# One fixed order of single steps for the front and the first tile, a third raw buffer, and low words on ScalarE

## The chip, the core and the metric

The kernel runs on one core of a Trainium2 chip. TensorE (PE) multiplies matrices, VectorE (DVE), ScalarE (ACT) and GpSimd (POOL) work on tiles in SBUF, and SyncE (SP) issues all the DMAs. The metric is the device time of one launch in microseconds (us), lower being better.

## The reference

Two layers. The first is an mLSTM: per batch and head a state `C` of 40 x 40 and a vector `n` are carried over 768 steps, with gates that are stabilised by a running maximum. The second is a feed-forward layer on its output, whose activation is the square of a clipped line.

```python
for t in range(S):                     # B, H, S, D = 4, 8, 768, 40
    m_new = np.maximum(f_gate[:, :, t] + m, i_gate[:, :, t])
    f_stab = np.exp(f_gate[:, :, t] + m - m_new)
    i_stab = np.exp(i_gate[:, :, t] - m_new)
    C = f_stab[..., None, None] * C + i_stab[..., None, None] * np.einsum('bhd,bhe->bhde', vt, kt)
    n = f_stab[..., None] * n + i_stab[..., None] * kt
    denom = np.maximum(np.abs(np.einsum('bhd,bhd->bh', n, qt)[:, :, None]), 1.0)
    y[:, :, t] = 1 / (1 + np.exp(-o_gate[:, :, t])) * np.einsum('bhde,bhe->bhd', C, qt) / denom
h = x @ w_in                           # x: 3072 x 320, w_in: 320 x 2048
g = np.where(h >= 1, h, np.where(h <= -1, 0.0, (h + 1) ** 2 / 4))
out = g @ w_out                        # 2048 x 320
```

The weights `w_in` and `w_out` arrive as 64-bit floats, and the kernel makes 32-bit floats of them from the raw words.

## The kernel before

Time is cut into 6 chunks of 128 steps, and 4 batches by 6 chunks make 24 **sequences** n = 0 to 23. Each goes through the attention: `prep` (mask and exponents of the decay matrix `Abc`, on POOL and ACT), `score` (q times k on PE, times the decay matrix on DVE, in two halves), `main` (a read of the state, the main product, the denominator `z`, the output `y`, its transposes, and its high and low parts `xh` and `xl`), and a carry that renews the state `C`. Four sequences give 512 tokens, one **tile** j of the feed-forward layer, of which there are 6. A tile has 16 blocks fc: `mm1` is the first product into a bank `psh` (8 matmuls on high and low parts), ACT makes `relu` and its square from it, DVE the largest of that and the bank (`r`), which frees the bank; there are two. `mm2` is the second product into four banks `pso`. In tile 0 it is a plain f32 product (`ow`, `r`); from tile 1 on it is one in three parts (`oh`, `ol`, `gh`, `gl`). Since `LAG` is 2, `mm2` of a block comes two blocks after its `mm1`.

The weights come in 16 parts, 8 of each, each for two blocks. `load_w` issues the load into a raw buffer `wraw` (two of them), and `convert` makes the floats: ACT shifts the magnitude (`mg`), DVE writes the sign (high half of `win` or `ow`), POOL the low words, DVE bounds `mg` and joins both; for w_in ACT then makes the high part `wh` and DVE the low part `wl`. The order `W_ORDER` (lines 431 to 435) runs one part of w_in ahead. `split_next` (line 788) converts a part whole, as `DUE` asks, and issues the load of the part after the next.

The **front** (lines 799 to 861) is written out in `STEPS`, a word for a step: a load (`L..`), filler matmuls on zeros (`w2`), scores (`s0`), exponents by halves (`x20`, `x21` for sequence 2), and the like. In it `InOrder` (line 71) keeps each engine's instructions in the order written. After the front the order on each engine is the scheduler's, which takes priorities from the program's order: `slot(i)` (line 727) runs the steps that the table `plan` has for block i, and `behind(...)` puts some of them after named instructions. SP issues DMAs strictly in its order; each uses one of eight semaphores in turn, so a DMA also waits for the eighth before it.

Of the kernel before, what the change touches and what calls it, by code (L numbers as in the profile page):

```python
# [34 lines left out]
PLAIN_FC = 16  # L35
# [5 lines left out]
EARLY = 8  # L41
# [5 lines left out]
JOINED = (4, 5, 6, 7)  # L47
ST = 0
# [3 lines left out]
DUE = lambda fc: 3 + fc  # L52
# [18 lines left out]
class InOrder:  # L71
# [7 lines left out]
    def __getattr__(self, name):  # L79
        def call(*args, **kwargs):  # L80
            if not InOrder.on or self.last is None:
# [17 lines left out]
def mlstm_ffn_kernel(ctx, tc, qk, qn, vk, og, fi0, fi, fib, w_in, w_out, cst, out):  # L99
# [83 lines left out]
    def load_batch():  # L183
        mb["row"] = mid.tile([NSEQ, 2, 4 * L], F32, name="fi_r")
# [14 lines left out]
    def batch_sums():  # L199
        a, m = mb["fi"][:, 0, :], mb["m"]  # L200
        ah = mb["ah"] = mid.tile([P, L], F32, name="ah_b")
        ac = mb["ac"] = mid.tile([P, L], F32, name="ac_b")
# [169 lines left out]
    def words(out, raw):  # L372


# [4 lines left out]
        out = out.rearrange("p k f -> p (k f)").bitcast(I32)  # L379
        halves = out.bitcast(U16).rearrange("p (f w) -> p f w", w=2)  # L380
# [18 lines left out]
    def load_w(kind, i):  # L399
        if kind == "in":  # L400
            n = 2 * P
            raw = stage.tile([P, 3, 2 * n], I32, name="wraw", bufs=2)
            at = nc.sync.dma_start(raw.rearrange("p k f -> p (k f)"), w_in[i])
        else:
            raw = stage.tile([P, 2, 2 * DM], I32, name="wraw", bufs=2)
# [4 lines left out]
    def convert(kind, i):  # L410
        raw = raws.pop((kind, i))
        if kind == "in":
            sl = slice(2 * i * P, 2 * (i + 1) * P)
            w = stage.tile([P, 3, 2 * P], F32, name="win", bufs=1)
            words(w, raw)
            yield
            yield from split(wh[:, :, sl], wl[:, :, sl], w)
        else:
            of[i] = ow.tile([P, 656], F32, name="ow")[:, :2 * DM].rearrange("p (k e) -> p k e", k=2)
            words(of[i], raw)  # L420
            if 2 * i >= PLAIN_FC:
                yield
                yield from split_out(i)
# [114 lines left out]
    def prep(n):  # L538

        c, b = divmod(n, B)  # L540
        t = T[n]
        select(n)
        if n not in JOINED:
            yield
# [4 lines left out]
        scale1(n)  # L549
        load_v(n + 1)  # L550
        yield
# [58 lines left out]
    def carry_on(n, t):  # L610

        c, b = divmod(n, B)
        kp = psum_a()
        for gi, h0 in enumerate(GROUPS):
            nc.tensor.matmul(kp[0:120, gi * 3 * D1:(gi + 1) * 3 * D1], t["kn"][:, h0 * D:(h0 + 3) * D],
                             t["v2"][:, h0:h0 + 3, :], start=True, stop=True)
        Cn = st.tile([120, 3, 3 * D1], F32, name="C", bufs=5)
# [3 lines left out]
        if c > 0:  # L621
            C = state[b]
            nc.gpsimd.tensor_tensor(out=C, in0=C, in1=dec[:, :, b, c:c + 1].broadcast_to([120, 3, 3 * D1]),
                                    op=ALU.mult)
            nc.vector.tensor_tensor(out=Cn, in0=Cn, in1=C, op=ALU.add)
        state[b] = Cn

    def first(n):

        load_v(n)  # L630
        scale2(n)
        yield
        carry_on(n, T.pop(n))
        yield

    def main(n):

        c, b = divmod(n, B)
        t = T.pop(n) if n >= B else T[n]
        g = gates_of(n)  # L640
        sg = sig[c][:, b, :]
        M = t["A"]
        if c > 0:
            C = state[b]
            ip = psum_a()
            for gi, h0 in enumerate(GROUPS):
                o = 6 - h0 if gi == 2 else 0
                nc.tensor.matmul(ip[:, (h0 + o) * D1:(h0 + 3) * D1], t["qn"][:, gi, :], C[:, gi, o * D1:3 * D1],
                                 start=True, stop=True)
            hv = wk.tile([P, H, D1], F32, name="hv", bufs=2)  # L650
            iv = ip[:, :H * D1].rearrange("p (h d) -> p h d", d=D1)
            nc.vector.tensor_tensor(out=hv, in0=iv, in1=g[:, 2, :].unsqueeze(2).broadcast_to([P, H, D1]), op=ALU.mult)
        up = psum_a()
        hot(up)
        if n < SPLIT_FROM or b == B - 1:
# [13 lines left out]
        uv = up[:, :H * D1].rearrange("p (h d) -> p h d", d=D1)  # L669
        if c > 0:  # L670
            nc.vector.tensor_tensor(out=hv, in0=uv, in1=hv, op=ALU.add)
        else:
            hv = uv
        if n >= B:
            load_A(n + NA)
        yield
# [4 lines left out]
        nc.vector.reciprocal(out=z, in_=z)  # L681
        sz = wk.tile([P, H, D], F32, name="sz", bufs=1)
# [4 lines left out]
        if 0 < c < NC - 1:  # L687
            carry_on(n, t)
# [7 lines left out]
        if c == 0:  # L696
            yield
# [6 lines left out]
        mark["x", "act"] = nc.scalar.copy(xh[:, :, cs], xv)  # L704
# [266 lines left out]
```

## Time and profile before

| what | value |
|---|---|
| median of 3 runs | 518.27 us (517.52 to 518.61) |
| span of the profiled execution | 516.2 us |
| busy: PE, DVE, ACT, POOL | 490.7, 343.0, 289.1, 135.9 us |
| chain that ended last | PE 85%, DVE 6%, ACT 5%, DMA 3% |
| idle of ACT's relu for PE, of DVE's largest for ACT | 111.4, 71.3 us |
| one load: w_in part, w_out part, decay matrix, gate sig | 768, 640, 512, 640 KB |
| one load: half of q and k, v and k, q | 160, 324, 180 KB |

The span runs from the first to the last instruction, and the timed runs take in a little around it. Busy PE time is not PE at its peak, since matmuls are pipelined and their ends are modelled; so the time from the start of one group to the start of the next tells more than a duration. Nearly all instructions are recorded by the helper `InOrder` and stand on its lines 82 and 85; the tiles tell them apart. Times are counted from the span's start.

### The profile page before, as it was taken

How to read it: one execution, taken by the hardware profiler on the slowest of the kernel's cores; microseconds unless marked ns; L12 is line 12 of the kernel's file. 1: busy time of each engine (PE TensorE's matmuls, PEld its weight loads, DVE VectorE, ACT ScalarE, POOL GpSimd, SP SyncE). 2: the span in 40 equal slices, each digit the busy share in tenths (PEclk: the TensorE clock that was granted, in tenths of full speed). 3: DMA queues.
4: the chain of work that ended last, by engine and by line, in shares of the span. 5: the costliest groups of instructions: out<-in, count | busy, mean ns of one | idle time of the engine just before them, and what ended most of it. 6: DMA issues, size and time to landing. Idle time of an engine off the chain costs nothing.

```text
span 516.2 us, 8817 instructions
## 1 busy us (share of the span) xinstructions
PE 490.7 (95%) x3396; PEld 419.4 (81%) x3399; DVE 343.0 (66%) x621; ACT 289.1 (56%) x560; POOL 135.9 (26%) x136
## 2 busy tenths in 40 slices
PE   8985999889898999999999998999999999999996
PEld 3763877778677989988889988889888889988986
DVE  4789896679758776759696657756756745444332
ACT  4525884436087555676645567555377554455553
POOL 2324531343433333323142314403230210000000
PEclk8987999979999999999999999999999999999999
DMA  8868664364441303323223423113522000010001
GB/s 227 257 183 307 161 189 138 115 193 150 131 146 40 107 27 96 118 66 111 65 78 83 133 80 118 68 53 96 170 81 77 16 1 1 0 52 1 1 2 51
DMA packets 29646, 51.48 MB, mean 100 GB/s; under 512 B 10060, under 2 KB 19940, under 8 KB 29604
## 3 DMA queue, kind: packets, MB, share of 16 engines
q1 hardware_dynamic: 29604, 50.92, 32.4%
q8 instruction: 27, 0.44, 0.4%
q14 instruction: 15, 0.12, 0.1%
HBM read 46.80 MB, written 4.04 MB: 98 GB/s over the span
## 4 chain that ended last, share of the span: by engine, by line
PE 85%; DVE 6%; ACT 5%; DMA 3%; issue 1%; SPq 0%; ACTq 0%; DVEq 0%
PE pso L82 33%; PE psh L82 33%; PE psa L82 15%; ACT Abc L82 1%; PE pso L85 1%; DMA raw<-in_qk 1%; ACT L82 1%; PE psa L85 1%; DVE ow L82 1%; DMA wraw<-in_w_in 1%; PE psh L85 1%; ACT r L82 1%; DVE win L82 1%; DMA out<-r 1%; ACT sig L82 0%
## 5 line engine op out<-in xcount | busy, mean ns | idle before, releaser
L82 ACT ACTIVATE r<-psh,half 128x512 f32<-128x512 f32 x96 | 65.4, 685 | 111.7 <-PE psh L82 111.4
L82 DVE SCALAR_TENSOR_TENSOR r<-psh,r 128x512 f32<-128x512 f32 x96 | 65.8, 686 | 71.5 <-ACT r L82 71.3
L82 PE MATMUL psh<-xh,wh 128*128 128x512 f32 x288 | 104.3, 418 | 6.7 <-DVE r L82 6.1
L82 PE MATMUL pso<-oh,gh 128*128 128x320 f32 x320 | 100.6, 317 | 2.4 <-ACT gh L82 2.1
L82 PE MATMUL psh<-xh,wl 128*128 128x512 f32 x288 | 99.8, 401 | 0.0
L82 PE MATMUL pso<-ow,gh 128*128 128x320 f32 x320 | 99.2, 312 | 0.0
L82 PE MATMUL pso<-oh,gl 128*128 128x320 f32 x320 | 94.0, 311 | 1.6 <-DVE gl L82 1.6
L82 DVE TENSOR_TENSOR gl<-r,gh 128x512 fp32r<-128x512 f32 x80 | 62.2, 779 | 40.5 <-ACT gh L82 40.4
L82 ACT CAST gh<-r 128x512 fp32r<-128x512 f32 x80 | 49.4, 618 | 51.0 <-DVE r L82 50.4
L82 PEld LDWEIGHTS pso<-oh,gh 128*128 128x128 f32 x320 | 60.1, 188 | 7.4 <-ACT gh L82 2.5
L82 PEld LDWEIGHTS psh<-xh,wl 128*128 128x128 f32 x288 | 55.2, 192 | 13.1 <-DVE wl L85 0.4
L82 PEld LDWEIGHTS psh<-xh,wh 128*128 128x128 f32 x288 | 51.8, 194 | 15.2 <-DVE r L82 6.8
L82 PEld LDWEIGHTS pso<-ow,gh 128*128 128x128 f32 x320 | 60.2, 188 | 2.8
L82 PE MATMUL psh<-xl,wh 128*128 128x512 f32 x192 | 62.3, 405 | 0.0
L82 ACT ACTIVATE r<-r 128x512 f32<-128x512 f32 x96 | 60.4, 632 | 2.5
L82 PEld LDWEIGHTS pso<-oh,gl 128*128 128x128 f32 x320 | 58.9, 188 | 2.1 <-DVE gl L82 1.9
L82 ACT ACTIVATE Abc<-Abc,nA 128x128 f32<-128x128 f32 x160 | 49.9, 391 | 0.2
L82 POOL TENSOR_TENSOR v<-vk,G 128x328 f32<-128x328 f32 x36 | 30.6, 856 | 58.3 <-issue 45.9
L82 PEld LDWEIGHTS psh<-xl,wh 128*128 128x128 f32 x192 | 36.8, 192 | 8.6
L82 PE MATMUL pso<-ow,r 128*128 128x320 f32 x128 | 38.5, 443 | 0.5 <-DVE ow L82 0.5
L82 POOL TENSOR_SCALAR_AFFINE_SELECT Abc<-Abc 128x1024 f32<-128x1024 f32 x20 | 25.4, 1275 | 48.3 <-DMA Abc<-a_d 46.1
L82 POOL TENSOR_TENSOR m<-m 128x1024 bf16<-128x1024 f32 x12 | 24.4, 2037 | 46.4 <-DVE m L82 46.4
(203 smaller groups left out, 681.0 us busy)
## 6 DMA issues: line engine op xcount, KB each, us to landing
Abc<-a_d SPq DMA_DIRECT2D x20, 512.0 KB
raw<-in_qk SPq DMA_DIRECT2D x48, 160.0 KB
vk<-in_vk SPq DMA_DIRECT2D x20, 324.0 KB
wraw<-in_w_in SPq DMA_DIRECT2D x8, 768.0 KB
wraw<-in_w_out SPq DMA_DIRECT2D x8, 640.0 KB
sig<-in_og SPq DMA_DIRECT2D x6, 640.0 KB
out<-r SPq DMA_DIRECT2D x24, 160.0 KB
qn<-in_qn SPq DMA_DIRECT2D x20, 180.0 KB
```

Source lines behind the costliest of these rows:

```text
L82: r = getattr(self.engine, name)(*args, **kwargs)
L85: r = getattr(self.engine, name)(*args, **kwargs)
```

## The change

The written order goes on to the end of tile 0. `STEPS` gets some 250 words more, such as `mm.2`, `relu.2`, `max.2`, `out.2` for the steps of a block, `w.1` for the next single step of the conversion of weight part 1, `W.3` for a load, `carry.0`, `prep.4`, `score.4`, `main.4` for the next step of a sequence's; the generators now yield after nearly each instruction. `--` stands where the banks of tile 0 are taken. Low words go from POOL to ACT, `wraw` has three buffers, the parts alternate between w_in and w_out, and two small tiles of the gates (`ah`, `ac`) share a buffer with `fi_r`. The main loop begins at tile 1, whose steps by block are the same in number and place.

```diff
+    "w2 E3 A3 x30 e v2.0 w2 s3 v3 w.1 y1 x31 t0 m30 m31 w2 u2 z1 y2 w2 v.1 u3 v.3 t1 z2 qk.4 v2.1 w.2 W.3 y3 w2 "
+    "v.2 t2 z3 qk.5 w.2 og.1 v2.3 w.2 W.4 t3 d g1 -- A.4 v2.2 carry.0 carry.3 A.5 mm.0 mm.1 w.2 relu.0 w.2 carry.3 "
+    "w.3 w.3 max.0 carry.1 prep.4 tail.1 w.2 carry.0 carry.1 out.0 v.4 W.5 relu.1 carry.2 A.6 w.2 w.3 w.3 sig.1 "
...
-    def words(out, raw):
+    def words(new, raw):
...
         nc.scalar.activation(mg, hi.bitcast(F32), AF.Abs, scale=65536.0)
+        yield
+        out = new().rearrange("p k f -> p (k f)").bitcast(I32)
+        halves = out.bitcast(U16).rearrange("p (f w) -> p f w", w=2)
+        nc.scalar.activation(halves[:, :, 0], quarter[:, :, 1], AF.Copy, scale=1 / 8192, bias=-4095.5 / 8192)
+        yield
+        nc.vector.tensor_scalar_max(mg, mg, TINY)
+        yield
         nc.vector.tensor_scalar(out=halves[:, :, 1], in0=quarter[:, :, 3], scalar1=0x8000, scalar2=None,
                                 op0=ALU.bitwise_and)
-
-        nc.gpsimd.tensor_scalar(out=halves[:, :, 0], in0=quarter[:, :, 1], scalar1=1 / 8192, scalar2=-4095.5 / 8192,
-                                op0=ALU.mult, op1=ALU.add)
-        nc.vector.tensor_scalar_max(mg, mg, TINY)
+        yield
         nc.vector.scalar_tensor_tensor(out=out, in0=mg.bitcast(I32), scalar=3, in1=out,
                                        op0=ALU.logical_shift_left, op1=ALU.bitwise_or)
+        yield
...
-            raw = stage.tile([P, 3, 2 * n], I32, name="wraw", bufs=2)
+            raw = stage.tile([P, 3, 2 * n], I32, name="wraw", bufs=3)
...
-    W_ORDER = [("in", 0)]
-    for i in range(NFC // 2):
-        if i + 1 < NFC // 2:
-            W_ORDER.append(("in", i + 1))
-        W_ORDER.append(("out", i))
+    W_ORDER = [(kind, i) for i in range(NFC // 2) for kind in ("in", "out")]
...
+    def tile0(what):
+        kind, n, *_ = what.split(".") + [0]
+        n = int(n)
+        if kind == "mm":
+            block[n] = mm1(0, n)
+        elif kind == "relu":
+            gs[n] = relu(block[n])
+        elif kind == "max":
+            gs[n] = largest(block[n], gs[n]),
+        elif kind == "out":
+            mm2(ops[0], n, *gs.pop(n))
+        elif kind == "w":
+            weights(n)
+        elif kind == "W":
+            load_w(*W_ORDER[n])
...
+        else:
+            step(kind, n)
...
+    def weights(k, i=1):
+        if k not in convs:
+            convs[k] = convert(*W_ORDER[k])
+        for _ in range(i):
+            next(convs[k], None)
...
-    for x in range(NG + LAG):
+    for x in range(NFC, NG + LAG):
```

ACT in the front, from the gate exponents on (`Abc_307`, `Abc_315`: decay matrix of sequence 2; `A3`: of sequence 3; `wraw_161`: the second raw buffer). Before:

```order
L85 ACTIVATE mg_278<-wraw_147 128x768
L85 ACTIVATE Abc_307<-pso_308,nA_122 128x128 x4
L85 ACTIVATE Abc_307<-pso_309,nA_122 128x128 x4
L85 ACTIVATE A3_368<-psh_369,nA_122 128x128 x4
L85 CAST wh_131<-win_277 128x3x256
```

And after the change:

```order
L98 ACTIVATE mg_285<-wraw_147 128x768
L98 ACTIVATE win_287<-wraw_147 128x768
L98 ACTIVATE mg_322<-wraw_161 128x640
L98 ACTIVATE Abc_315<-pso_316,nA_122 128x128 x4
L98 ACTIVATE ow_356<-wraw_161 128x640
L98 ACTIVATE Abc_315<-pso_317,nA_122 128x128 x4
L98 CAST xh_382<-psa_378 128x3x128
L98 ACTIVATE A3_385<-psh_386,nA_122 128x128 x4
L98 CAST wh_131<-win_287 128x3x256
```

The first pass over part 0 of w_out moved ahead of the exponents of sequence 2, and its low words between their halves; `wraw_161` now holds that part, where it held part 1 of w_in.

SP in tile 0, around the twelve DMAs of the decay factors (`dec`); `dc_d` is what they read, `vk_695` and `qn_697` belong to sequence 5, `wraw_707` is part 3 of w_out after the change. Before:

```order
L82 DMA dc_d_124<-dx_b_566 128x40
L82 DMA wraw_635<-in_w_out 128x1280
L82 DMA wraw_685<-in_w_in 128x1536
L82 DMA dec_125<-dc_d_124 120x4x1 x12
L82 DMA wraw_738<-in_w_out 128x1280
```

And after the change:

```order
L98 DMA Abc_618<-a_d_120 128x1024
L98 DMA dc_d_124<-dx_b_632 128x40
L98 DMA dec_125<-dc_d_124 120x4x1 x12
L98 DMA vk_695<-in_vk 128x648
L98 DMA qn_697<-in_qn 120x384
L98 DMA wraw_707<-in_w_out 128x1280
```

Two weight loads stood between the store and the twelve, and now none; three loads, one of weights, follow the twelve.

ACT in tile 0, where it comes to that part (`r_869`: relu of block 5; `Abc_549`: sequence 5), after the change:

```order
L98 CAST wh_131<-win_795 128x3x256
L98 ACTIVATE mg_849<-wraw_707 128x640
L98 ACTIVATE ow_863<-wraw_707 128x640
L98 ACTIVATE Abc_549<-Abc_549,nA_122 128x128 x4
L98 ACTIVATE r_869<-psh_807,half_118 128x512
L98 ACTIVATE r_869<-r_869 128x512
```

Both passes over the part stand ahead of the second half of the exponents of sequence 5 and of a relu; before, a part's low words were on POOL.

## Rows read from the trace of the kernel before

**Rows 1.** By stretches: us, busy time of each engine, PE clock, DMA share, GB/s

```profile
37.00:47.00 10.00, 3.88 (x13) 2.81 (x13) 9.79 (x19) 4.84 (x8) 4.06 (x4) 0.83 0.71 221
...
97.00:107.00 10.00, 6.86 (x57) 5.84 (x57) 8.30 (x16) 5.94 (x13) 2.93 (x4) 0.91 0.59 179
...
437.00:457.00 20.00, 20.00 (x120) 18.21 (x119) 9.11 (x19) 9.28 (x16) 0.00 (x0) 1.00 0.00 0
```

**Rows 2.** Timeline of PE: start, us, instruction, count, idle time before and releaser

```profile
33.56 2.07 PE L82 MATMUL psh<-xh,wh 128*128 128x512 f32 x4 [0.57 <-ACT xh L85]
...
45.20 1.22 PE L82 MATMUL psh<-xh,wh 128*128 128x512 f32 x2 [6.12 <-DVE r L82]
...
67.36 0.73 PE L82 MATMUL psh<-xh,wh 128*128 128x512 f32 x2
...
97.24 1.16 PE L82 MATMUL psa<-raw 40*128 40x128 f32 x14
...
143.00 0.71 PE L82 MATMUL psh<-xh,wh 128*128 128x512 f32 x2
```

**Rows 3.** Chain that ended last: one first product, one second product of tile 0

```profile
51.96 1.86 PE psh L82 x8
...
58.90 2.15 PE pso L82 x8
```

**Rows 4.** Timeline of PE: state read, main product, carry, next first product

```profile
118.89 0.80 PE L82 MATMUL psa<-C,qn 120*128 120x123 f32 x6
119.52 1.92 PE L82 MATMUL psa<-v,Abc 128*128 128x41 f32 x16
121.26 0.87 PE L82 MATMUL psa<-v,vk 128*120 128x123 f32 x6
121.89 1.18 PE L82 MATMUL psh<-xh,wh 128*128 128x512 f32 x4
```

**Rows 5.** Timeline of ACT in the front: exponents of sequence 2

```profile
17.70 2.17 ACT L85 ACTIVATE Abc<-pso,nA 128x128 f32<-128x128 f32 x8 [2.00 <-PE pso L85]
```

**Rows 6.** Timeline of DVE in the front

```profile
21.13 1.28 DVE L85 TENSOR_TENSOR Abc<-pso,Abc 128x512 f32<-128x512 f32 x2
...
26.46 0.42 DVE L85 TENSOR_TENSOR xl<-psa,xh 128x256 fp32r<-128x256 f32 x1 [2.50 <-ACT xh L85]
...
33.54 0.42 DVE L85 TENSOR_TENSOR xl<-psh,xh 128x256 fp32r<-128x256 f32 x1 [0.51 <-ACT xh L85]
...
34.30 0.96 DVE L85 TENSOR_TENSOR wl<-win,wh 128x768 fp32r<-128x768 f32 x1
```

**Rows 7.** Timeline of SP's issues: start, us until the last is issued

```profile
14.30 0.35 SPq L85 DMA_DIRECT2D wraw<-in_w_in  x1
...
19.66 3.55 SPq L82 DMA_DIRECT2D raw<-in_qk  x2
...
56.54 7.69 SPq L82 DMA_DIRECT2D dec<-dc_d  x12
64.39 0.36 SPq L82 DMA_DIRECT2D wraw<-in_w_out  x1
```

**Rows 8.** Waits of SP's queue up to 60 us: total, times, longest

```profile
SPq L82 <- DMA wraw<-in_w_in: 3.0, 1, 3.0
```

**Rows 9.** Timeline of POOL: the low words of a w_out part

```profile
68.50 0.92 POOL L82 TENSOR_SCALAR ow<-wraw 128x640 uint16<-128x640 uint16 x1 [3.18 <-DMA wraw<-in_w_out]
```

**Rows 10.** Groups of instructions from 33 to 147 us: count, busy us, mean ns, idle before

```profile
L82 DVE SCALAR_TENSOR_TENSOR ow<-mg,ow 128x640 int32<-128x640 int32 x8 | 9.9, 1237 | 0.2
...
L82 ACT ACTIVATE mg<-wraw 128x768 f32<-128x768 f32 x7 | 6.4, 918 | 1.3 <-DVE ow L82 1.3
L82 ACT ACTIVATE mg<-wraw 128x640 f32<-128x640 f32 x8 | 6.3, 791 | 0.0
...
L82 POOL TENSOR_SCALAR win<-wraw 128x768 uint16<-128x768 uint16 x7 | 8.9, 1271 | 20.3 <-DVE mg L82 7.4 <-DVE wl L82 7.4 <-DMA wraw<-in_w_in 3.3
...
L82 POOL TENSOR_SCALAR ow<-wraw 128x640 uint16<-128x640 uint16 x8 | 7.8, 974 | 25.5 <-DMA wraw<-in_w_out 25.4
```

More of the change, by code (lines that the diff above doesn't have):

```diff
@@ L183, in load_batch @@
     def load_batch():
-        mb["row"] = mid.tile([NSEQ, 2, 4 * L], F32, name="fi_r")
+        mb["all"] = mid.tile([P, 2, 4 * L], F32, name="fi_r")
+        mb["row"] = mb["all"][:NSEQ]
         nc.sync.dma_start(mb["row"], fi[:, :, L:5 * L])
@@ L413, in convert, with new @@
             sl = slice(2 * i * P, 2 * (i + 1) * P)
[L414 to L417, printed above, removed]
-        else:
[L419 to L423, printed above, removed]
+            w = []
+            def new():
+                w.append(stage.tile([P, 3, 2 * P], F32, name="win", bufs=1))
+                return w[0]
+            yield from words(new, raw)
+            yield from split(wh[:, :, sl], wl[:, :, sl], w[0])
+        else:
+            def new():
+                of[i] = ow.tile([P, 656], F32, name="ow")[:, :2 * DM].rearrange("p (k e) -> p k e", k=2)
+                return of[i]
+            yield from words(new, raw)
     def split_out(i):
@@ L621, in carry_on @@
         if c > 0:
+            yield
             C = state[b]
@@ L724, in mlstm_ffn_kernel, with step @@
-    order = {"first": first, "score": score, "main": main, "prep": prep}
+    for n in range(2 * B, NS):
+        s0 = FRONT + OFFS[n - B]
+        todo = ("prep", s0 - LEAD - 1, (1, 1, 1, 0)), ("score", s0, (2, 1)), ("main", s0 + MLAG, (4, 2, 3))
+        for kind, i0, steps in todo:
+            for i, k in enumerate(steps):
+                plan.setdefault(i0 + i, []).append((n, kind, i, k))
+    order = {"score": score, "main": main, "prep": prep, "carry": carry_on}
     gens = {}
+    def step(kind, n):
+        if (n, kind) not in gens:
+            gens[n, kind] = order[kind](n)
+        return next(gens[n, kind], None)
@@ L727, in slot @@
     def slot(i):
-        for n, kind in sorted(plan.get(i, ()), key=lambda x: (list(order).index(x[1]), x[0])):
-            if (n, kind) not in gens:
-                gens[n, kind] = order[kind](n)
-            next(gens[n, kind])
+        for n, kind, at, k in sorted(plan.get(i, ()), key=lambda x: (list(order).index(x[1]), x[0])):
             c, b = divmod(n, B)
-            if kind == "main":
-                at[n] = at.get(n, 0) + 1
-                if b == 0 and at[n] == 1:
+            for m in range(k):
+                step(kind, n)
+            if kind == "prep" and at == 3:
+                scale1(n)
+                load_v(n + 1)
+            if kind == "score" and at == 0:
+                load_qk(n + 2)
+            if kind == "score" and at == 1 and c < NC - 1:
+                scale2(n)
+            if kind == "main" and at == 0:
+                load_A(n + NA)
+                if b == 0:
@@ L736, in slot @@
                     with behind(("r", "act")):
                         sigmoid(c)
-                if b == B - 1 and at[n] == 1 and c + 1 < NC:
+                if b == B - 1 and c + 1 < NC:
                     load_og(c + 1)
-    at = {}
+            if kind == "main" and at == 1 and 0 < c < NC - 1:
+                for _ in range(4):
+                    step("carry", n)
     def mm1(j, fc):
@@ L784, in store @@
             nc.sync.dma_start(out[row(NTC * j + t) * L:(row(NTC * j + t) + 1) * L, :], o)
[L786 to L796 removed]
+    NG = B * S // TT * NFC
+    ops = {}
+    gs = {}
+    block = {}
+    def tile0(what):
[13 more added lines that the diff above has]
+            load_w(*W_ORDER[n])
+        elif kind == "og":
+            load_og(n)
+        elif kind == "sig":
+            sigmoid(n)
+        elif kind == "v":
+            load_v(n)
+        elif kind == "qk":
+            load_qk(n)
+        elif kind == "A":
+            load_A(n)
+        elif kind == "v1":
+            scale1(n)
+        elif kind == "v2":
+            scale2(n)
+        elif kind == "tail":
+            batch_tail()
+        elif kind == "exps":
+            batch_exps()
+        else:
+            step(kind, n)
+    convs = {}
+    def weights(k, i=1):
[3 more added lines that the diff above has]
+            next(convs[k], None)
     InOrder.on = True
[L800 removed]
     for what in STEPS.split():
         n = int(what[1]) if what[1:2].isdigit() else 0
[L804 to L805 removed]
+        hh = int(what[2:]) if what[2:].isdigit() else 0
+        if "." in what:
+            tile0(what)
+        elif what == "--":
+            front = False
+            gates.close()
+            mo = ctx.enter_context(tc.tile_pool(name="mo", bufs=2))
+            ops[0] = [ps_o.tile([P, 512], F32, name="pso") for _ in range(NTC)]
+        elif what == "Lg":
             first_gates()
```

133 lines of the change are left out of this document (34 added, 99 removed), and 19 rows, old and new, of the table STEPS.

## The prediction

> **What bounds the kernel now.** Four views, in this order. First the table by stretches [rows 1]: from 437 us on TensorE (PE) is busy for all of a 20 us stretch, and the page's PE line reads 9 in nearly every slice from the twelfth on. Tiles 1 to 5 are therefore bound by PE, and a tile that starts earlier ends earlier. In two stretches before that PE is far from full: 3.88 of 10 us from 37 us on, where VectorE (DVE) is busy for 9.79, and 6.86 of 10 from 97 us on. Second, PE's timeline [rows 2]: the first product of tile 0 starts at 33.56, PE then sits idle for 6.12 us before 45.20 until DVE has released a result bank, and the first product of tile 1 starts at 143.00. So tile 0 with the attention work between takes 109.4 us. Third, what that work is worth when nothing waits [rows 3, 4]: a first product of a block (8 matmuls) 1.86 us, a second product of tile 0 (4 plain f32 matmuls, shown as 8) 1.9 to 2.15, a score 1.1 to 1.2, a state read 0.63 (118.89 to 119.52), a main product 1.74, a carry 0.63. Sixteen of each product, five scores and five reads, four main products, eight carries, four groups of transposes at 0.33 and the gate transposes at 0.4 make 29.8 + 32.5 + 5.5 + 3.2 + 7.0 + 5.0 + 1.3 + 0.4 = 84.7 us (2.03 for a second product). Thus 24.7 of the 109.4 us are no work. Even the densest stretch, 67.36 to 97.24 [rows 2], holds 6 + 6 products and 4.8 us of attention, 28.2 us in 29.9: about 6% is lost there too, 5.1 us on 84.7. **At most 19.6 us** are there to win, all of it ahead of tile 1.
>
> **The change, part by part.** (a) ScalarE (ACT) writes the low words in place of GpSimd (POOL). POOL loses 15 instructions in tile 0, 8.9 + 7.8 = 16.7 us [rows 10]; it is no bound there. ACT gains as many. No row shows such an ACT instruction; its nearest rows are ACT's own passes over the same raw words, 918 and 791 ns, which make 7 x 0.92 + 8 x 0.79 = 12.8 us; the far end is POOL's 1271 and 974 ns, 16.7 us. I take the first, being the same engine and size. Cheaper than that would gain nothing where PE is the bound. The cover is PE work; without it each is on ACT's path to the next relu.
>
> (b) The weights in turn. PE's order changes at the start of tile 0: carries and the first second-product stand ahead of the third first-product, so that less waits for the second part of w_in. DVE worked without a break from 34.30 to 45.20 [rows 2, 6] and needed 10.9 us from the first part's low half to the second relu; after, the conversion of out part 0 (1.24 us for its longest step [rows 10], some 2.3 in all) lies in the front, and three carries (1.6) and more of the gate sums stand in its place. I put that list at 9.7 us.
>
> (c) The front. The conversion of out part 0 now runs there. ACT waits for that load ahead of the exponents of sequence 2 (the fences on ACT in the front, in the section on the change). Its place in SP's queue is that of the second w_in load of before, issued at 14.30. When that landed is seen on SP: the second DMA of the pair at 19.66 was held 3.0 us by it and went out at 22.9 [rows 7, 8]. So 768 KB landed 8.6 us after its issue, the queue filling the time before; 640 KB in the same place would land near 22.3. In the trace those exponents start at 17.70 [rows 5]. After, ACT starts its first pass at 22.3, the first half of the exponents at 23.1, then the low words (0.75), and ends the second half at 26.1. Behind it on ACT stand the copy of x of sequence 0, the exponents of sequence 3 and the wh copy; DVE waits for both halves. DVE had 21.13 to 34.27 for its list to the last x part, 3.0 us of it idle (2.50 and 0.51) [rows 6]: 10.1 us of work, 1.8 with the new steps added to that: 11.9. Of these 1.2 can be done ahead of 26.1; 26.1 + 10.7 = 36.8, with half a us for hand-overs 37.3: **3.1 us later** than 34.27. The two ends: 0, if the load lands by 17.7, and 5.3, if nothing of the lateness is caught up. PE uses part of it, since two carries run ahead of the first product: its work starts at 36.1, not 33.56.
>
> The Trainium skill (DMA: Bandwidth & Descriptors, Queues, rings and completion order) says that completion is not first in, first out per issuing engine. If the load of out part 0 could land ahead of those issued earlier, the 3.1 would vanish and the sum be 505.8; what rows show are landings in the order of issue [rows 7, 8].
>
> (d) The third raw buffer. The first load that it takes is w_in part 3, read only after six other parts; until then two buffers go round as before. It puts 768 KB ahead of w_in part 1 in the queue, about 3 us at the 240 GB/s (768 KB between 19.7 and 22.9) seen there [rows 7, 8]. Part 1 then lands near 31.5, and is needed from about 34: hidden.
>
> (e) SP's queue behind the decay factors. Twelve small DMAs held SP from 56.54 to 64.23 [rows 7]. After, they stand straight behind the store of dx, and out part 3 behind them (the fences on SP). In the trace a load issued behind them at 64.39 was read at 68.50 [rows 9]: 4.1 us. ACT reaches dx late after the change, near 50.5, since the sigmoid with two table loads stands ahead of it; the store lands behind three 512 KB loads and an out part, near 59; the twelve end near 67, out part 3 lands near 71 to 72. ACT wants it at 65.5 by its list. Queued behind that wait are the second half of the exponents of sequence 5 and the relu of product 5; what DVE makes of the two frees the bank for product 7 and the one for the carry. PE has work until then; I take **4.5 us** of its time, ends 0 and 6.5.
>
> The sum. PE's work starts at 36.1. To the third first-product at 47.0 (37.3 + 9.7) it has 8.7 us of work in 10.9: 2.2 us of waits. Then 1.0 us while the fifth score waits for banks that DVE frees, 4.5 of (e), 1.4 where the eleventh second-product waits for its weights, and 6% of the 62 us left, 3.7. 36.1 + 84.7 + 2.2 + 1.0 + 4.5 + 1.4 + 3.7 = **133.6** for the first product of tile 1, 9.4 ahead of 143.00. Tiles 1 to 5 keep their work and order: nothing for them. The span would be 516.2 - 9.4 = 506.8. The profile gives the execution's span alone; the median of the runs, 518.27, lies 2.1 above it, so **508.9**.
>
> **Rivals.** *The waits do not come.* If the load in (c) is early enough and SP is through its twelve before ACT asks, 3.1 and 4.5 go: 518.27 - 17 = 501.3. For it speaks that in the trace the stretch behind the same twelve DMAs, from 67.36 on, is PE's densest [rows 2, 7]; against it that then POOL waited for the weights, not ACT, which also serves PE. *ACT becomes the bound and it ends slower.* ACT's list in tile 0 grows by 12.8 us while the time for it shrinks by 9. Every weight part is now read by ACT first, and a late part holds relus, exponents and copies behind it. Eight parts are loaded after out part 3; each us that each is late beyond its cover is one us of PE. If they are late by over 1.2 us each, the 9.4 are gone; at 2 us each the time is 518.27 - 9.4 + 16 = 524.9. Against it: three buffers from then on, and some 13 MB in 73 us by the sizes in the profile's table, under 180 GB/s, where 240 were seen. *Given back.* With the low words at POOL's durations and half a us late per part, 4 + 4 us: 517 to 519, no change. *The change doesn't do what it says:* the third buffer is none for the first six parts (d); that is in the forecast.
>
> **How the numbers follow.** Forecast (503.5 to 515) 0.70; waits don't come (501.3, up to 503.5) 0.17; no change 0.06; slower by ACT 0.07. About 0.2% is what a measurement of this kernel can tell from no change. The first two and a sixth of the third are faster by over 0.2% (under 517.2): 0.88; within 0.05, slower 0.07. For 8 in 10 I leave out the lower part of the second case and the two last: 502 to 516.
>
> **What would show it.** Right: ACT idle near 16.5 to 22.3 until w_out's load, the last x part at 37, SP held by the twelve until 66 or later with ACT waiting for w_out just after, the first product of tile 1 at 131 to 136, tiles 1 to 5 unchanged at 373 us. Wrong: ACT without a wait in the front (the time is 3 us lower), ACT waiting for weights four times or more between 75 and 130 (no gain), or a stretch behind tile 1 that is longer than before.

## Result and profile after the change

The changed kernel takes **504.79 us** (median of 4 runs, 501.54 to 506.86), the kernel before 518.37 beside it (517.52 to 518.61): a ratio of 0.9738, 95% interval 0.9696 to 0.9779, 13.6 us less. The forecast was 508.9. The profiled run took 506.14 us with a span of 504.4, so 1.74 us lie around the span.

First the table by stretches, the same stretches as [rows 1] (columns as there):

```profile
37.00:47.00 10.00, 9.28 (x50) 6.99 (x49) 9.29 (x24) 7.22 (x10) 0.00 (x0) 0.98 0.44 149
97.00:107.00 10.00, 9.23 (x59) 7.33 (x59) 8.30 (x14) 8.23 (x20) 5.05 (x6) 1.00 0.41 132
437.00:457.00 20.00, 20.00 (x115) 18.12 (x113) 9.00 (x15) 11.33 (x20) 0.00 (x0) 1.00 0.10 34
```

From 37 us on TensorE (PE) is busy 9.28 us of 10 where it was 3.88, and 9.23 from 97 us on where it was 6.86. Late stretches are full as before. Now PE's timeline, which answers to [rows 2, 4] (start, us, instruction, count, idle time before it and what ended that):

```profile
36.84 1.67 PE L98 MATMUL psa<-ow 128*120 128x123 f32 x12
38.26 0.70 PE L98 MATMUL psh<-xh,wh 128*128 128x512 f32 x2
...
47.27 0.71 PE L98 MATMUL psh<-xh,wh 128*128 128x512 f32 x2
...
75.84 1.55 PE L98 MATMUL psa<-v,vk 128*120 128x123 f32 x6 [2.96 <-issue]
77.06 1.20 PE L98 MATMUL psh<-xh,wh 128*128 128x512 f32 x2
...
128.63 0.88 PE L98 MATMUL psh<-xh,wh 128*128 128x512 f32 x2
...
130.75 0.79 PE L98 MATMUL psa<-C,qn 120*128 120x123 f32 x6
...
133.41 0.86 PE L98 MATMUL psh<-xh,wh 128*128 128x512 f32 x2
...
135.50 0.22 PE L98 MATMUL psa<-v,Abc 128*128 128x41 bf16 x2
...
135.62 2.40 PE L98 MATMUL pso<-ow,r 128*128 128x320 f32 x8
```

The two carries start at 36.84, the first product of tile 0 at 38.26 and the third at 47.27. The idle time of 6.12 us before the third product [rows 2] is gone; the one large gap is 2.96 us before 75.84. The last second product of tile 0 ends at 138.02 (135.62 + 2.40). Before it stand two first products of tile 1, of 2.12 us (128.63 to 130.75) and 2.09 us (133.41 to 135.50). Without them tile 0 would be done at 133.8; that stands against 143.00 in [rows 2] and is **9.2 us earlier**. Behind that point the kernel before needs 516.2 - 143.00 = 373.2 us, the changed one 504.4 - 133.8 = 370.6: **2.6 us less in tiles 1 to 5**. Together 11.8, the difference of the spans.

PE's own share of those two stretches, before and after (columns as in [rows 1]):

```profile
33.56:143.00 109.44, 98.26 (x494) 76.14 (x495) 88.03 (x143) 56.36 (x108) 41.87 (x40) 0.92 0.57 176
36.84:138.02 101.18, 96.53 (x523) 75.31 (x523) 81.29 (x147) 73.17 (x133) 24.74 (x24) 0.96 0.55 174
```

PE's work starts 3.3 us later and it is idle for 4.7 us where it was 11.2. Without the two products of tile 1 it is busy for 92.3 us where it was 98.3, for the same work: 11.2 - 4.7 + 98.3 - 92.3 - 3.3 = 9.2. So the waits are only one half of the win. Part of the other half is the clock, which was low for 17.5 us of the stretch before and for 8.1 of the one after (2 x (1 - granted clock) x stretch); how much of the 6.0 us that is, no run takes apart.

ACT's timeline, in the front and at w_out part 3, answers to [rows 5]:

```profile
21.37 0.79 ACT L98 ACTIVATE mg<-wraw 128x640 f32<-128x640 f32 x1 [5.79 <-DMA wraw<-in_w_out]
22.06 1.14 ACT L98 ACTIVATE Abc<-pso,nA 128x128 f32<-128x128 f32 x4
...
72.02 0.77 ACT L98 ACTIVATE mg<-wraw 128x640 f32<-128x640 f32 x1 [5.33 <-DMA wraw<-in_w_out]
...
73.48 1.25 ACT L98 ACTIVATE Abc<-Abc,nA 128x128 f32<-128x128 f32 x4
```

Both waits of the forecast are there: 5.79 us for w_out part 0 ahead of the exponents of sequence 2, which start at 22.06 and not at 17.70, and 5.33 us for w_out part 3. SP's timeline says why the second one is long; it answers to [rows 7]:

```profile
51.01 0.33 SPq L98 DMA_DIRECT2D dc_d<-dx_b  x1
56.64 7.05 SPq L98 DMA_DIRECT2D dec<-dc_d  x12
...
64.81 0.35 SPq L98 DMA_DIRECT2D wraw<-in_w_out  x1
```

The store of dx is issued at 51.01, the twelve small DMAs hold SP until 63.69 (56.64 + 7.05), and w_out part 3 is issued at 64.81; ACT reads it at 72.02. Then come the exponents of sequence 5 (73.48), and DVE's product with them:

```profile
75.06 0.68 DVE L98 TENSOR_TENSOR Abc<-psa,Abc 128x512 f32<-128x512 f32 x1
```

That product reads a `psa` bank and ends at 75.74; PE's carry into `psa` starts at 75.84. The trace names no releaser for PE's gap of 2.96 us, so that the bank ends it is read from this order.

Groups of instructions from 33 to 147 us, which answer to [rows 10] (count, busy us, mean ns, idle before):

```profile
L98 ACT ACTIVATE win<-wraw 128x768 uint16<-128x768 uint16 x7 | 7.5, 1071 | 1.8 <-DVE wl L98 1.8
...
L98 ACT ACTIVATE ow<-wraw 128x640 uint16<-128x640 uint16 x7 | 6.4, 920 | 0.0
...
L98 DVE SCALAR_TENSOR_TENSOR ow<-mg,ow 128x640 int32<-128x640 int32 x7 | 5.8, 822 | 0.5
```

POOL's low words (1271 and 974 ns) are gone, ACT's take 1071 and 920 ns. And VectorE (DVE) is faster: its longest step of a w_out part takes 822 ns where it took 1237, with the same operands.

### The profile page after: what moved, and what is told of

Its sections match the earlier page's. It is cut to its first block, busy times and chain, and to the rows that moved or that the text cites. A ratio compares the mean times of both kernels' runs of the same rounds, so it can differ in the third digit from the quotient of the medians.

```text
span 504.4 us, 8805 instructions
## 1 busy us (share of the span) xinstructions
PE 488.2 (97%) x3396; PEld 419.2 (83%) x3399; DVE 338.5 (67%) x621; ACT 303.0 (60%) x576; POOL 112.8 (22%) x120
## 4 chain that ended last, share of the span: by engine, by line
PE 74%; ACT 4%; DVE 1%; issue 0%; ACTq 0%
PE pso L98 31%; PE psh L98 30%; PE psa L98 13%; ACT Abc L98 1%; ACT L98 1%; ACT r L98 1%; ACT sig L98 1%; DVE y L98 0%; ACT gh L98 0%; DVE gl L98 0%; DVE r L98 0%; DVE sz L98 0%; DVE z L98 0%; ACTq L997 0%; DVE v L98 0%
## 5 line engine op out<-in xcount | busy, mean ns | idle before, releaser
L98 PE MATMUL psh<-xh,wh 128*128 128x512 f32 x288 | 101.5, 406 | 0.0
L98 PE MATMUL psh<-xh,wl 128*128 128x512 f32 x288 | 99.8, 398 | 0.4 <-DVE wl L98 0.4
L98 PE MATMUL pso<-oh,gl 128*128 128x320 f32 x320 | 95.6, 312 | 0.0
L98 PEld LDWEIGHTS psh<-xh,wh 128*128 128x128 f32 x288 | 50.5, 190 | 6.5 <-DVE r L98 0.2
```

## Experiments

Each kernel is the changed one with the edit shown, unless it says otherwise, and was timed beside the kernel before. In the edits the text is the list of steps: w.1 is the next step of converting w_out part 0, W.7 the load of w_out part 3, dec.1 the twelve DMAs as a step of its own, w4 four filler products ahead of the next group on PE. In a cut edit `...` stands for steps left out. The columns of the table behind the ratio are each from the trace of one run of the kernel: the time in which the granted clock was 1.2 GHz during the first 46 us (2 x (1 - granted clock) x 46, from the table by stretches), the start of the first product, the time from there to the end of the last second product of tile 0, and PE's gaps between 70 and 86 us. In the kernel before and in e11_before_act tile 0 holds 16 first products, in the others 18, two of them (some 4.2 us) of tile 1.

| kernel | median us | ratio to before, 95% | low clock, us | first product | tile 0 | gaps |
|---|---|---|---|---|---|---|
| before | 518.1 to 518.9 | 1 | 9.2 | 33.56 | 106.5 | none |
| changed | 504.79 | 0.9696 to 0.9779 | 10.1 | 38.26 | 99.8 | 2.96 |
| after_again | 503.49 | 0.9651 to 0.9750 | 20.2 | 41.05 | 96.3 | 2.52 |
| e1_front | 505.04 | 0.9668 to 0.9773 | 10.1 | 39.10 | 97.6 | 2.23 |
| e2_dec | 505.90 | 0.9698 to 0.9798 | 17.5 | 41.66 | 97.0 | 1.07, 2.02 |
| e3_both | 504.58 | 0.9666 to 0.9764 | 10.1 | 38.78 | 96.4 | 1.10, 1.63 |
| e5_front2 | 504.02 | 0.9681 to 0.9758 | 10.1 | 37.98 | 97.5 | 2.70 |
| e6_heat | 502.31 | 0.9640 to 0.9721 | 13.8 | 40.60 | 97.5 | 2.61 |
| e7_dec2 | 502.35 | 0.9654 to 0.9727 | 13.8 | 38.65 | 97.2 | 2.26 |
| e8_all | 501.52 | 0.9640 to 0.9730 | 0 | 35.26 | 97.0 | 2.22 |
| e9_best | 503.26 | 0.9672 to 0.9743 | 6.4 | 40.31 | 95.5 | 1.54 |
| e10_pool_out | 510.79 | 0.9786 to 0.9870 | 10.1 | 39.70 | 103.8 | 1.92 |
| e11_before_act | 519.51 | 1.0017 to 1.0084 | 6.4 | 32.96 | 107.2 | none |
| e12_third | 503.34 | 0.9655 to 0.9733 | 23.9 | 42.41 | 98.4 | 2.38 |

The runs of one kernel lie 3 to 8 us apart, so differences of 1 to 2 us between these medians are not settled. The traced run was the slowest of its six in after_again, e2_dec, e6_heat, e7_dec2, e9_best and e12_third, so the traces show where time goes, not which variant is faster. e10_pool_out and e11_before_act stand clear of the rest.

**The changed kernel again,** without an edit, for the spread.

> The changed kernel, unchanged, beside the others on one chip. Its runs so far went from 501.5 to 506.9 us with mean granted clocks of 0.983 to 0.992. Theory: the spread is the clock's, and the median stays within 0.5% of 504.8. Rival: the spread was one chip's, and here the runs lie within 0.3% of each other.

Runs from 501.05 to 505.54 us: the spread is there on this chip too, and the first product of the profiled run starts 2.8 us later than in the first profile, with 10 us more of low clock. Behind the last second product of tile 0 both need the same, 366.4 us (504.4 - 138.02) and 366.5 (503.8 - 137.32). What differs between the two lies in the front and in tile 0, and it nearly cancels: the second starts tile 0 2.8 us later and takes 3.5 us less for it. Ten us more of low clock in the front did not make it the slower one; the first trace has a low stretch behind the gap at 75.84 instead.

**The front without ACT's wait.** Two forms. In the first ACT's two steps moved behind the first half of the exponents of sequence 3, and DVE's three behind them, the first of these still ahead of the result of sequence 1 (`y1`):

```
-E2 w.1 A2 x20 w2 s2 y0 w.1 x21 v2 w.1 m20 m21 w2 u1 w.1 z0 w2 E3 A3 x30 e v2.0 w2 s3 v3 w.1 y1 x31 t0 m30 m31 w2 u2 z1
+E2 A2 x20 w2 s2 y0 x21 v2 m20 m21 w2 u1 z0 w2 E3 A3 x30 e w.1 w.1 v2.0 w2 s3 v3 w.1 y1 x31 t0 w.1 m30 m31 w2 u2 w.1 z1
```

> The changed kernel with the conversion of w_out part 0 placed later in the front: ACT's two passes over it stand behind the first half of the exponents of sequence 3, so ACT no longer waits for that load (landing near 21.4) ahead of the exponents of sequence 2. Theory (step c): those exponents start near 18 and not at 22.06, the last x part of tile 0 is done near 35 and not at 38.3, and the end comes 3 to 4 us earlier than the changed kernel's (near 501). Rival: the front ends earlier, but VectorE's list up to the third first-product, now with the conversion's long step later in it, sets the place of that product all the same: at most 1 us is won.

The exponents of sequence 2 start at 16.09, but the first product starts at 39.10. At DVE's first step DVE waited for ACT:

```profile
26.45 0.49 DVE L98 TENSOR_SCALAR mg<-mg 128x640 f32<-128x640 f32 x1 [4.38 <-ACT mg L98]
```

So the second form moved all of DVE's steps behind that result:

```
+E3 A3 x30 e v2.0 w2 s3 v3 y1 x31 t0 m30 m31 w.1 w.1 w2 u2 z1 w.1 y2 w2 v.1 u3 v.3 w.1 t1 z2 w.1 qk.4
```

> The changed kernel with the whole conversion of w_out part 0 later in the front: ACT's two passes stand behind both halves of the exponents of sequence 3, VectorE's three steps between the steps of sequences 2 and 3, so that neither engine waits for that load ahead of the results of sequences 1 and 2. In the first form of this edit only ACT's steps moved, and VectorE, in its fixed order, waited 4.38 us for ACT's pass instead. Theory (VectorE's and ACT's place in the order set the front): the last x part is done near 35 to 36 in place of 38.3, the first product starts near 36, and the time is 2 to 3 us below the changed kernel's of the same chip. Rival (TensorE's clock sets the front): the first product still starts anywhere between 38 and 42, by where in the front the granted clock falls to 0.50, and the time is within 1 us.

Neither ACT nor DVE waits for the load any more, and still the first product starts at 37.98, as in the changed kernel at the same 10.1 us of low clock. PE and POOL, from their timelines, show what is late instead:

```profile
30.32 2.92 PE L98 MATMUL psa<-ow,A 128*128 128x41 f32 x16 [2.06 <-POOL ow L98]
...
37.98 0.70 PE L98 MATMUL psh<-xh,wh 128*128 128x512 f32 x2
```

```profile
28.59 3.65 POOL L98 TENSOR_TENSOR ow<-ow,G 128x328 f32<-128x328 f32 x4 [11.30 <-DMA ow<-in_vk]
```

```profile
16.57 0.33 SPq L98 DMA_DIRECT2D wraw<-in_w_in  x1
18.92 0.33 SPq L98 DMA_DIRECT2D ow<-in_vk  x1
```

PE waits 2.06 us for POOL's scaling of v of sequence 3. In POOL's fixed order (v2.0 ahead of v3 in the list) that stands behind a product for sequence 0. SP issues that product's load at 18.92, behind parts of the weights, the third buffer's early one among them, and POOL can start only at 28.59, 9.7 us later. In the changed kernel the same POOL group starts at 28.97, but PE comes so late that the wait does not show. The time is the rival's, within 1 us; but besides the clock that the rival named, the removed wait was replaced by one standing right behind it. v3 ahead of v2.0 was not tried. Runs at equal clock say the same: at a mean granted clock of 0.989 to 0.990 four runs of the changed kernel took 501.05 to 503.57 us, the one of e1_front 502.39 and the one of e5_front2 502.08.

**PE's clock in the front.** The second form with filler where PE sat idle:

```
-w2 u1 z0 ... w2 u2 z1 w.1 y2 w2 v.1 u3 v.3 w.1 t1 z2
+w2 u1 w4 z0 ... w2 u2 w4 z1 w.1 y2 w8 v.1 u3 v.3 w.1 t1 w3 z2
```

> The kernel of e5_front2 with 17 more filler products (zeros, 128x512) on TensorE in the front, put where it sat idle in the traces: 4 ahead of the transposes of sequence 1, 4 and 3 ahead of those of sequences 2 and 0, 6 ahead of the output of sequence 3. Theory (the clock sets the front): the granted clock stays at 1.00 from 20 us to 38 us where it stood at 0.50 for some 10 us, the outputs of sequences 2 and 3 take 1.9 us each in place of 3.0 and 3.5, and the time is 2 to 4 us below the changed kernel's, with a smaller spread. Rival: the filler (about 0.22 us each at full clock) stands on the path and costs what it gives, or the clock falls all the same: within 1 us or 1 to 3 us slower.

502.31 beside 504.02 of e5_front2; the intervals overlap, so the gain of the edit is not settled. In the profiled run the clock was low from 9 to 22.5 us, mostly ahead of the added filler, and full from 24 to 38. But the twelve runs of e6_heat and e8_all, which have the same front, can be set beside their own mean granted clock: five at 0.999 or 1.000 took 499.27 to 502.35 us (mean 500.6), seven at 0.986 to 0.997 took 501.52 to 506.32 (mean 503.8). The profile of e8_all is of a run without low clock; the rows are its table by stretches (granted clock: the third number from the end) and PE's timeline up to tile 0:

```profile
0.00:46.00 46.00, 41.54 (x288) 28.79 (x289) 34.62 (x91) 27.36 (x56) 9.42 (x23) 1.00 0.78 246
```

```profile
29.96 1.98 PE L98 MATMUL psa<-ow,A 128*128 128x41 f32 x16 [1.40 <-POOL ow L98]
...
35.26 0.71 PE L98 MATMUL psh<-xh,wh 128*128 128x512 f32 x2
```

The first product starts at 35.26. The output of sequence 3 takes 1.98 us there, and 2.92 in e5_front2 above.

**The twelve DMAs later.** They become a step of their own, behind the loads of v of sequence 5 and of w_out part 3:

```
-score.4 prep.4 relu.2 w.4 v.5 out.1 prep.4 W.7 carry.2
+score.4 prep.4 relu.2 w.4 v.5 out.1 prep.4 W.7 dec.1 carry.2
```

> The changed kernel with the twelve DMAs of the decay factors taken out of the step that stores dx and placed behind the load of w_out part 3 (and of v, k and q of sequence 5), so that SP issues that load without waiting for the store. Theory (step e): the load is issued near 53 and lands near 58 to 60, ACT's wait of 5.33 us ahead of its first pass over it is gone, TensorE's idle 2.96 us near 73 to 76 and the low clock behind it (a first product of 3.56 us in place of 1.87) are gone too: 3 to 4.5 us less than the changed kernel. Rival: the twelve then hold the loads of raw of sequence 6 and of w_in part 4, ACT waits there instead, and the time is within 1 us of the changed kernel's.

> Both edits. Theory: the two waits stand in different places of one path, so the gains add: 6 to 8.5 us less than the changed kernel, near 497. Rival: another queue (VectorE's list in tile 0, or the next weight part) is late next, and both together win no more than the larger alone, 3 to 4 us.

505.9 and 504.6: nothing won, and e2_dec's chain of waits is the rival's, ACT waiting 5.79 us for w_in part 4. The same from the trace of e3_both, ACT and PE:

```profile
75.83 0.90 ACT L98 ACTIVATE mg<-wraw 128x768 f32<-128x768 f32 x1 [5.45 <-DMA wraw<-in_w_in]
```

```profile
73.81 0.87 PE L98 MATMUL psa<-v,vk 128*120 128x123 f32 x6 [1.10 <-issue]
...
80.66 1.98 PE L98 MATMUL psa<-v,Abc 128*128 128x41 f32 x16 [1.63 <-DVE hv L98]
```

ACT's wait is as long as before, for w_in part 4 in place of w_out part 3. PE's one gap became two, of 1.10 and 1.63 us, the second ended by DVE. SP itself was held: the load of v and k of sequence 5, ahead of all that, was issued only at 58.20, when PE had read the buffer it goes to. So the next edit put the next three weight loads ahead of the twelve, two of them ahead of that load too:

```
-w.3 v2.4 mm.3 ... w.4 v.5 out.1 prep.4 W.7 carry.2 score.4 relu.3 main.4 qk.6 w.4 W.8 max.2 A.7 w.4 ... W.9 w.4
+w.3 W.7 v2.4 mm.3 ... w.4 out.1 prep.4 carry.2 score.4 relu.3 main.4 w.4 W.8 v.5 max.2 w.4 ... W.9 dec.1 qk.6 A.7 w.4
```

> The changed kernel with SP's order around the decay factors rewritten: behind the store of dx the loads of w_out part 3 and w_in part 4, then v, k and q of sequence 5, then w_out part 4, and only then the twelve DMAs. In e2_dec the load of v and k of sequence 5, held until 58.2 us by TensorE's last reader of its buffer, stood ahead, and the twelve ahead of w_in part 4, for which ACT then waited 5.45 us. Theory: ACT waits for no weight part between 60 and 85 us (by over 1 us), TensorE's gap of 2.5 to 3.0 us there is gone, and the time is 2.5 to 4 us below the changed kernel's. Rival: TensorE is held there by VectorE's list all the same (2.02 us behind VectorE in e2_dec), and the time is within 1 us.

(The 58.2 and 5.45 us in it are e3_both's; e2_dec has 61.05 and 5.79.) ACT's wait for weights is gone in this stretch, as the theory wants. PE's gap is not: 2.26 us, and now POOL ends it.

```profile
74.84 0.87 PE L98 MATMUL psa<-v,vk 128*120 128x123 f32 x6 [2.26 <-POOL v L98]
```

```profile
72.24 0.80 POOL L98 TENSOR_TENSOR C<-C,dec 120x369 f32<-120x369 f32 x1 [14.61 <-DMA dec<-dc_d]
73.00 1.73 POOL L98 TENSOR_TENSOR v<-vk,G 128x328 f32<-128x328 f32 x2
```

POOL stood 14.61 us for the decay factors, and the scaling of v that PE waits for is queued behind that product. The rival named DVE; it was POOL. Both front and this edit together:

> The edits of e6_heat and e7_dec2 together. Theory: they stand in different stretches and add up, 4.5 to 8 us below the changed kernel, near 497. Rival: tile 0 is bound by VectorE's list from the front on, and the two together win no more than one, 2 to 4 us.

501.52, the lowest median of all; its gap is e7_dec2's (2.22), and the two edits do not add to 4.5 us. The last edit moved POOL's product behind the scalings, and put four more filler products ahead of the first scores (`w6 s0` for `w2 s0`), so its front is not e8_all's:

```
-main.4 carry.4 w.6 v1.5 ... score.5 v2.5 w.7
+main.4 w.6 v1.5 ... score.5 v2.5 carry.4 w.7
```

> The kernel of e8_all with two more edits: POOL's product of the state with the decay factors (the third step of the carry of sequence 4) stands behind both scalings of v of sequence 5, so that these don't wait for the twelve DMAs, and 4 more filler products stand ahead of the first scores. In e7_dec2 and e8_all TensorE waited 2.26 and 2.22 us near 72 to 75 us for POOL's scaling of v, which stood behind that product. Theory (three engines waited in turn for the one chain of store, twelve DMAs and product, and this is the last of them): TensorE has no gap of over 0.5 us between 60 and 85 us, and the time is 1.5 to 2.5 us below e8_all, near 499.5. Rival: a fourth wait stands there, and the time is within 1 us of e8_all.

```profile
68.20 1.68 POOL L98 TENSOR_TENSOR v<-vk,G 128x328 f32<-128x328 f32 x2 [8.46 <-DMA vk<-in_vk]
74.04 0.80 POOL L98 TENSOR_TENSOR C<-C,dec 120x369 f32<-120x369 f32 x1 [4.16 <-DMA dec<-dc_d]
```

```profile
74.88 0.55 DVE L98 TENSOR_TENSOR C<-C 120x369 f32<-120x369 f32 x1 [1.84 <-POOL C L98]
```

```profile
76.12 0.86 PE L98 MATMUL psa<-v,vk 128*120 128x123 f32 x6 [1.54 <-issue]
```

POOL's scalings are early (68.20). Now DVE waits 1.84 us for the product, the next engine in turn, and PE's gap is 1.54. Tile 0 is the shortest of all, 95.5 us, but 503.26 does not beat e8_all: the rival. Its front, 40.31 with 6.4 us of low clock, had PE idle 2.66 us for POOL's scaling of v of sequence 3; and behind tile 0 the traced run took 368.0 us where that of e8_all took 366.4, at a granted clock of 0.98 to 0.99 between 250 and 350 us where the other had 1.00.

**Where the low words are made.** In the changed kernel's order, the w_out parts back on POOL:

```
+if n == 640:
+    nc.gpsimd.tensor_scalar(out=halves[:, :, 0], in0=quarter[:, :, 1], scalar1=1 / 8192, scalar2=-4095.5 / 8192, ...)
+else:  (ACT's line, as it was)
```

> The changed kernel with the low words of the eight w_out parts back on GpSimd, those of w_in left on ACT; all else in the changed kernel's order. ACT has 7.4 us less to do in tile 0 (8 at 0.92), POOL 7.6 us more. Theory (step a: ACT's added work lies beside TensorE's): within 1 us of the changed kernel, 502.5 to 505. Rival (ACT's list sets tile 0): 2 to 5 us faster than it. Other rival (POOL's steps hold what is queued behind them there): 2 us or more slower.

510.79, some 6 us slower than the changed kernel's 503.5 to 504.8: the second rival. POOL, DVE, ACT and PE at the place, in the order in which the wait goes on:

```profile
98.79 1.09 POOL L98 TENSOR_SCALAR_AFFINE_SELECT Abc<-Abc 128x1024 f32<-128x1024 f32 x1 [8.15 <-DMA Abc<-a_d]
99.97 0.90 POOL L98 TENSOR_SCALAR ow<-wraw 128x640 uint16<-128x640 uint16 x1
```

```profile
100.90 0.82 DVE L98 SCALAR_TENSOR_TENSOR ow<-mg,ow 128x640 int32<-128x640 int32 x1 [5.49 <-POOL ow L98]
```

```profile
101.76 0.90 ACT L98 ACTIVATE mg<-wraw 128x768 f32<-128x768 f32 x1 [6.91 <-DVE ow L98]
```

```profile
103.38 1.22 PE L98 MATMUL psh<-xh,wh 128*128 128x512 f32 x2 [5.48 <-DVE r L98]
```

POOL waited 8.15 us for a load of the attention (a_d); the low words queued behind it, DVE's step behind those (5.49), ACT's next part behind that (6.91) and PE's next product behind a relu (5.48). The low words themselves take 0.90 us. And the same move alone, in the kernel before:

```
-nc.gpsimd.tensor_scalar(out=halves[:, :, 0], in0=quarter[:, :, 1], ...)
+nc.scalar.activation(halves[:, :, 0], quarter[:, :, 1], AF.Copy, scale=1 / 8192, bias=-4095.5 / 8192)
```

> The kernel before with one edit: the low words of the fifteen parts behind the front (and of the first) on ACT in place of GpSimd, everything else, the planner of tile 0 too, as before; the planner gives tile 0 another order for it. Theory: the order written out by hand made the gain, not the place of the low words: within 2 us of the kernel before, 516 to 520. Rival: the low words on ACT alone take out the waits of tile 0: 510 or less.

519.51, 0.2 to 0.8% slower than before: the theory. The gap ahead of the third product is still there, as in [rows 2], if shorter:

```profile
42.70 0.95 PE L82 MATMUL psh<-xh,wh 128*128 128x512 f32 x2 [4.25 <-DVE r L82]
```

**The third buffer in turn.**

```
-w2 s0 W.6 x01 m00 ... m01 W.2 w2 ... w.2 W.3 y3 ... v.4 W.5 relu.1
+w2 s0 x01 m00 ... m01 W.2 W.3 w2 ... w.2 y3 ... v.4 W.5 W.6 relu.1
```

> The changed kernel with the third raw buffer given to the parts in turn: the early load of w_in part 3 moved behind that of w_out part 2, and the load of w_out part 1 moved up to straight behind that of w_in part 1, so that each part is loaded one place earlier. Theory (step d: those parts are in time with two buffers, so the third does nothing for the first six): within 1 us of the changed kernel. Rival: the third buffer used from the start takes 1 to 3 us out of the first 35 us of tile 0; other rival: w_in part 3, now loaded near 50 us, is late and costs 1 us or more.

503.34 beside 503.49 (another chip): no difference that can be measured. Its profile is of a run of 509.1 us, the longest of six, with 23.9 us of low clock; the first product starts at 42.41 in it, the latest of all.

## Why the prediction was right, and where it was not

Judged against the profiled run, the errors are: tiles 1 to 5 take 2.6 us less (forecast 0), tile 0 is done 9.2 earlier (forecast 9.4), and 1.74 us lie around the span, not 2.1. 508.9 - 2.6 + 0.2 - 0.4 = 506.1, the run's time. The median is another 1.3 lower, since that run is one of the slower two of four. The first product of tile 1 itself starts at 128.63, earlier than the 131 to 136 of the forecast, since PE takes two of them ahead of the last second products of tile 0; 133.8 is the mark that answers to the 133.6 of the sum.

*The ceiling and the bound.* The win lies ahead of tile 1 for the most part, as said; that half of it would be less busy time for the same work is in the sum only as the 6% of loss, and the clock, low for 8.1 us in place of 17.5, has no term of its own. **Tiles 1 to 5 gaining nothing was the wrong step.** The 373 us were taken as PE's own work, but PE is busy for 363.7 of them, before and after; in the rest it waited 2.7 us at the start of tile 1 (its waits in the kernel before, 143 to 175 us: total, times, longest), and after the change, from 134 to 166 us, it does not:

```profile
PE pso L82 <- DVE gl L82: 1.6, 1, 1.6
PE psa L82 <- DVE hv L82: 0.6, 1, 0.6
PE pso L82 <- ACT gh L82: 0.5, 1, 0.5
```

```profile
PE psa L98 <- issue: 0.2, 1, 0.2
```

That DVE and ACT come to tile 1 with a shorter backlog is the likely cause, but not shown; which edit does it was not taken apart. The low words alone do not: e11_before_act needs 377.1 us behind its last second product, the kernel before 376.2.

*(a) The low words.* The price was too low: 1071 and 920 ns, 14.9 us in all and not 12.8. That ACT's work lies beside PE's held, since the whole stretch is as full as it is. But "Cheaper than that would gain nothing" missed two things. DVE's seven steps of conversion cost less per part: for seven w_in and seven w_out parts 44.2 us of DVE before and 35.4 after (the sums of the groups, seven eighths of those with eight). In the kernel before the same step is seen at both prices; DVE's and POOL's timelines:

```profile
65.68 0.80 DVE L82 SCALAR_TENSOR_TENSOR ow<-mg,ow 128x640 int32<-128x640 int32 x1
...
81.44 1.66 DVE L82 SCALAR_TENSOR_TENSOR ow<-mg,ow 128x640 int32<-128x640 int32 x1
```

```profile
81.42 1.07 POOL L82 TENSOR_SCALAR win<-wraw 128x768 uint16<-128x768 uint16 x1 [4.21 <-DVE mg L82]
```

Alone it takes 0.80 us, beside POOL's low words 1.66. The Trainium skill (SBUF — State Buffer, Who interferes with whom) says that a VectorE instruction with two SBUF inputs contends with a GpSimd instruction that reads SBUF, and that the port pair they share is an exclusive lock; the trace agrees, 1.66 being 0.86 us longer, most of POOL's 1.07. And in a fixed order POOL's own waits for loads would stand ahead of the low words: some 6 us in e10_pool_out. In the kernel before the move alone makes nothing faster (e11_before_act), though the step comes down to 952 ns there; and in e10_pool_out, with POOL's low words of w_out back, it stays at 824, so how often the two meet is a matter of the order too.

*(b) The weights in turn.* Third first-product at 47.27 (forecast 47.0): the place was right, what sets it was not. The forecast had DVE's list set it, 9.7 us behind the last x part. That part was done at 38.3, not 37.3, and DVE had released the bank long before, at 43.75:

```profile
43.07 0.68 DVE L98 SCALAR_TENSOR_TENSOR r<-psh,r 128x512 f32<-128x512 f32 x1
```

PE's own work filled the stretch: 9.7 us of the 10.4 from 36.84 on, priced at 8.7, with waits of 0.7 us (0.39 and 0.34) in place of 2.2.

*(c) The front.* The event was right: ACT waited until 21.37 (forecast 22.3), and PE's work starts at 36.84 (36.1). **The reason was wrong**: with that wait taken out (e1_front, e5_front2) nothing comes earlier at the same total of low clock. The step that makes the last x part 3.1 us later out of ACT's wait (37.3 less 34.27 is 3.0) left out POOL, where the scaling of v of sequence 0 now stands ahead of that of sequence 3, and the granted clock, which is low for 0 to 23.9 us of the front with the first product at 35.26 to 42.41. The size came out near by chance. What ACT's wait would cost in a front that keeps the full clock is open: the one trace of such a front (e8_all) is without that wait.

*(d) The third buffer.* Right: e12_third, where it goes round from the start, takes the same time.

*(e) The twelve DMAs.* SP held to 63.69 (forecast 67, and 66 or later as the sign), ACT stopped until 72.02 (71 to 72), though the load took 7.2 us from its issue and not 4.1: two errors that cancel. PE idle 2.96 us with about 2.4 more at the lower clock behind it (a first product of 3.56 us from 77.06, a carry of 1.22); forecast 4.5. The event was right; the idle time alone is two thirds of the 4.5, and the rest is a cost of the clock that the forecast did not have. That the time would come back without ACT's wait, as the first rival has it, is not so: the waiting engine changes (ACT, ACT and DVE, POOL, DVE), the gap goes from 2.5 to 3.0 down to 1.5. As far as the traces name them, all hang on one chain: store of dx, twelve DMAs, product of the state or the loads behind the twelve.

*The other terms.* The waits of 1.0 (fifth score) and 1.4 us (eleventh second-product) did not come, one of 0.77 did (103.42). From 36.84 to 133.8 are 97.0 us. Less the 84.7 of work, 4.7 of gaps (0.39, 0.34, 0.20, 2.96, 0.77) and 2.6 of lower clock (2.4, and 0.2 in the first carries) that leaves 5.0 of loss inside the dense stretches, forecast 3.7. So the sum of 133.6 was met by errors of either sign. Of the sign "ACT waiting for weights four times or more" there was one wait between 75 and 130, 4.19 us before 113.34, and PE had no gap there. The 0.2% that the forecast took as the least change to be told was too small for this kernel: the interval of its own ratio is 0.8% wide.

*Completion order.* The rule of the Trainium skill cited with (c) (DMA: Bandwidth & Descriptors, Queues, rings and completion order) would have brought 505.8 by taking ACT's wait out of the front; the wait came, and e5_front2, without it, is not measurably lower (504.02 beside 503.5 to 504.8).

## What to carry to other kernels

Before a wait is costed as the time of the waiting engine, look at what stands at the same place on the other queues: here edits that removed a wait of over 5 us in full (e5_front2, e7_dec2) gained nothing that could be told from the spread, because another engine hung on the same chain or on the next load. In a fixed order an instruction inherits all that its queue waits for; here the idle POOL, whose queue waits for loads, was a worse place for the low words than the busy ACT (e10_pool_out). And compare versions that lie 1% apart over several executions with their granted clock beside them, not over one profile each.

## What the runs showed of the hardware

Executions of one kernel differ by where in the front PE's granted clock is at its lower level: 10.1 and 20.2 us in two profiles of the changed kernel, with the first product 2.8 us apart. Ahead of a fall PE had short gaps, 1.33 us before 21.16 and 0.80 us before 25.05 in the first profile, and the clock was down from about 27 on; in e8_all a gap of 1.40 us before 29.96 had no fall behind it. Of the twelve runs with one front, those with a mean granted clock of 0.999 or 1.000 took 500.6 us in the mean, the others 503.8. A VectorE step of 0.80 us took 1.66 beside a GpSimd instruction of 1.07.
